# Round 0 of a fused attention and MLP kernel, taken in two parts of 128 and 256 steps

## Chip, core and metric

The kernel runs on one core of one Trainium2 chip. The metric is the device time of one execution in microseconds. TensorE multiplies matrices, VectorE and ScalarE work elementwise and read its results out of PSUM, GpSimd (POOL in the profile) does elementwise work on SBUF, and SyncE (SP) issues most of the transfers.

## The reference

Two blocks one after the other. The first is a linear attention with a decay per channel (batch 4, 8 heads, 768 steps, 48 channels a head), the second a norm and an MLP with a residual:

```python
for t in range(S):
    kt, vt, rt, wt = (k[:, :, t], v[:, :, t], r[:, :, t], w[:, :, t])
    cur = np.einsum('bhd,bhe->bhde', u[None] * kt, vt)
    y[:, :, t] = np.einsum('bhd,bhde->bhe', rt, state + cur)
    state = wt[:, :, :, None] * state + np.einsum('bhd,bhe->bhde', kt, vt)
x = y.transpose(0, 2, 1, 3).reshape(B, S, H * D)      # 4 x 768 x 384
xn = (x - mu) / np.sqrt(var + 1e-06) * g_ln           # mu, var over the 384
out = x + np.maximum(xn @ w_ch1, 0.0) @ w_ch2         # 384 -> 1536 -> 384
```

All inputs and the output are float32.

## The kernel before

**Rounds.** The work is cut into eight rounds of 384 steps, two for each batch entry; the second continues the state of the first. A round has two units (`uu`) of four heads, and the heads of a unit go in two pairs: two heads of 48 channels share the 128 partitions, at rows 0 and 64. The 384 steps are three tiles of 128 (`TT = 3`), each of two chunks of 64.

**Attention of a round** (`front`). `load` fetches `w`, `k` and `r` with steps on partitions. `turn` transposes them on TensorE (`w_ps`, `k_ps`, `r_ps`) and ScalarE, in round 0 also VectorE, copies them to SBUF with channels on partitions. `totals` multiplies decays together by halves, 64 steps to 1 chunk, in six instructions (`tot`, `decay`). Then six levels follow. At level `lev`, `quads` multiplies keys by queries for the blocks of size 2^lev (tile `a`), `keep` copies the wanted squares of the result into `A` under a mask, and `grow` scales `k` and `r` by the decay of that level, so that the next level, or the states, can use them. Level n+1 can only start once `grow` of level n is done, so the levels of one round are a serial chain between TensorE and VectorE. After the last level, `turn_k` transposes the keys back (`kn_ps`), `states` multiplies them by `v` and VectorE scans over the chunks (`s`, `last`), `own` and `own_term` make the term with `u` (`rk`, `own`, `vo`), and `outputs` multiplies `A` by `v` and the states by `r`; VectorE adds both into `x`. `load_v` fetches `v` and makes a copy `vx` with its two halves of partitions exchanged.

**MLP of a round** (`back`). `normalize` takes mean and variance of each step, `turn_x` transposes the result (`xT_ps`) and ScalarE scales it into `xf`. `mlp` multiplies by `w_ch1` in twelve products (`h_ps`, three matmuls each), applies the relu, then multiplies by `w_ch2` into three output tiles (`o`). Round 0 does this in float32; later rounds use split factors in a faster format (`xhl`, `xd`, `wh`, `wl`, `d`), which `halve` makes from the weights. `convert` prepares each of 24 weight tiles from its raw form: three ScalarE instructions (into `w` or `ffn`, and `held` or `rest`) and two VectorE ones, a shift and a join (`CUSTOM_DVE_ANT_0` in the profile).

**What sets the order.** The work is not issued as the functions are called. Each `plan.add` registers one operation with its engine, an estimated cost, the tiles it reads and writes, and a priority (`pri`, smaller is sooner; `at(rnd, stage)` is 40 a round plus the stage). `Plan.order` runs a list schedule over these estimates and emits the instructions in the resulting order, engine by engine; each engine then executes strictly in that order. So every change of an operation's cost, size or priority can move other operations, in later rounds too. Some points matter below. An operation with `port` set is not placed beside one of the other of VectorE and GpSimd; every GpSimd operation has it. When the plan sees TensorE wait over 0.4 us in its first 90 us, it puts `idle` matmuls of zeros there, up to three times 128 columns each. Tiles come from a fixed number of homes by tag, and `banks` are PSUM banks.

In `before`, round 0 has all 384 steps as one piece; `quads` and `grow` are issued separately for the two units in this round only. Its loads are six transfers of 288 KB, each row 576 bytes, three on SyncE's queue and three on ScalarE's.

Of the kernel before, what the change touches and what calls it, by code (L numbers as in the profile page):

```python
# [9 lines left out]
F32 = mybir.dt.float32  # L10
# [55 lines left out]
class Plan:  # L66
# [31 lines left out]
    def add(self, eng, cost, fn, r=(), w=(), new=(), pri=0, lat=0.0, size=0, port=False, tiled=False, count=0):  # L98
        costs = {eng: cost} if isinstance(eng, str) else dict(zip(eng, cost))
        op = Op(len(self.ops), costs, fn, pri, lat, size, port or "POOL" in costs, tiled, count)  # L100
# [160 lines left out]
def kernel(  # L261
# [57 lines left out]
    def tile_(tag, name, shape, dtype=F32):  # L319
        if name in tiles:  # L320
            return tiles[name]
        if tag == "a":
            tiles[name] = a_homes[plan.place[name]]
            return tiles[name]
        if tag == "nat" and name.startswith("nat_"):
            tiles[name] = nat_homes[plan.place[name]]
            return tiles[name]
        pool = banks if tag == "b" else homes
        t = pool.tile(shape, dtype, tag=f"{tag}{plan.place[name]}", name=name)
        tiles[name] = t  # L330
        return t
# [11 lines left out]
    for q in both_units:  # L343
        plan.hold("vo", f"nat_r{q}")
        tile_("vo", f"nat_r{q}", [P, NH * ROW])
# [27 lines left out]
    for t in nat_homes:  # L373
        POOL.memset(t[:, NH * ROW :], 0.0)
# [33 lines left out]

    SRC = {"w": w, "k": k, "r": r}

    def load(nm, q, eng="SP", pri=None):
        b, f, g = units[q]
        name = f"nat_{nm}{q}"

        queue = SP if eng == "SP" else ACT

        def go():
            to = tile_("nat", name, None)
            if q // U < ROWS:
                queue.dma_start(  # L420
                    out=to[:, 0 : NH * ROW].rearrange("p (h x) -> p h x", h=NH),
                    in_=SRC[nm][b, ts(g, NH), ds(f * RN, RN)]
                    .rearrange("h (p c) d -> p h (c d)", p=P),
                )
                return
            for c in range(TT):
                queue.dma_start(
# [4 lines left out]
        if pri is None:  # L432
            pri = at(q // U, "wrk".index(nm))
        new = [] if nm == "r" and q in both_units else [("nat", name)]
        cost, size = (0.5, 0.8) if q // U < ROWS else (1.65, 1.2)
        plan.add(eng, cost, go, w=[name], new=new, pri=pri, lat=2.0, size=size)
# [4 lines left out]
    def turn(nm, q, pr, stage):  # L441
        rnd, uu = divmod(q, U)
        key = f"nat_{nm}{q}"
        name, ps = f"{nm}{rnd}", f"{nm}_ps{q}_{pr}"

        rows = rnd < ROWS

        def go():
            t = tile_("b", ps, [P, RN])
            for c in range(TT):  # L450
                if not rows:
                    both = by_tile(tiles[key])[:, c, ts(pr, 2)].rearrange("p j d -> p (j d)")
                    PE.transpose(t[0:PD, ts(c, P)], both[:, 0:PD], ident)
                    continue


                at_ = 2 * pr * ROW + c * D
                second, first = ds(at_ + ROW - HP, PD), ds(at_, HP)
                PE.transpose(t[0:PD, ts(c, P)], tiles[key][:, second], ident)
                PE.transpose(t[0:HP, ts(c, P)], tiles[key][:, first], ident)  # L460

        def keep(e="ACT"):
            to, ps_ = tile_(nm, name, [P, U, W])[0:PD, uu, ts(pr, RN)], tiles[ps][0:PD]
            if rows:
                to = to.rearrange("p (s c) -> p s c", c=TT)
                ps_ = ps_.rearrange("p (c s) -> p s c", c=TT)
            (DVE.tensor_copy if e == "DVE" else ACT.copy)(out=to, in_=ps_)

        new = [(nm, name)] if uu == pr == 0 else []
        plan.add(  # L470
            "PE", 0.66 if rows else 0.33, go, count=12 if rows else 6, r=[key, (name, uu, pr)], w=[ps],
            new=[("b", ps)] + new, pri=at(rnd, stage), lat=0.17,
        )
        plan.add(
            ("ACT", "DVE") if rnd == 0 else "ACT", (0.45, 0.5) if rnd == 0 else 0.45, keep,
            r=[ps], w=[(name, uu, pr)], pri=at(rnd, stage) + EVICT / 2,
        )

    def parts_of(name, us=both_units):
        return [(name, uu, pr) for uu in us for pr in pairs]  # L480

    def totals(rnd):
        tot, dec, wt = f"tot{rnd}", f"decay{rnd}", f"w{rnd}"
        sizes = [U * W >> (lev + 1) for lev in range(NLEV)]
        starts = [sum(sizes[:i]) for i in range(NLEV - 1)]
        costs = list(zip((1.0, 0.55, 0.4, 0.3, 0.25, 0.2), (1.5, 0.9, 0.58, 0.42, 0.34, 0.25)))
        for lev in range(NLEV):
            def go(e, lev=lev):
                if lev == 0:
                    tile_("tot", tot, [P, U * W])  # L490
                    tile_("decay", dec, [P, U * NM])
                pair = level_total(rnd, lev).rearrange("p (q two) -> p q two", two=2)
                BY[e].tensor_tensor(
                    out=level_total(rnd, lev + 1), in0=pair[..., 0], in1=pair[..., 1], op=ALU.mult
                )
            plan.add(
                EITHER, costs[lev], go,
                r=parts_of(wt) if lev == 0 else [(tot, lev)],
                w=[(tot, lev + 1)] if lev < NLEV - 1 else [dec],
                new=[("tot", tot), ("decay", dec)] if lev == 0 else [], pri=at(rnd, 6 + lev),  # L500
            )

    def level_total(rnd, lev):
        if lev == 0:
            return tiles[f"w{rnd}"].rearrange("p u t -> p (u t)")[0:PD]
        if lev == NLEV:
            return tiles[f"decay{rnd}"][0:PD]
        n = U * W >> lev
        return tiles[f"tot{rnd}"][0:PD, U * W - 2 * n : U * W - n]

    def own(q):
        rnd, uu = divmod(q, U)
        b, f, g = units[q]
        kk, kr = f"nat_k{q}", f"nat_r{q}"
        rk, o, row = f"rk{q}", f"own{rnd}", f"own_row{rnd}"
        rows = rnd < ROWS

        def parts():

            t = tile_("rk", rk, [P, NH * ROW])  # L520
            if rows:
                views = [
                    t_[:, 0 : NH * ROW].rearrange("p (h c d) -> p c h d", h=NH, c=TT)
                    for t_ in (tiles[kk], tiles[kr], t)
# [4 lines left out]
            return views + [u_bc[:, None, ts(g, NH)].broadcast_to([P, TT, NH, D])]  # L529
# [9 lines left out]
        def third():  # L539
            t = tile_("own_row", row, [P, TT, H]) if rows else tile_("own", o, [P, TT, H])  # L540
            DVE.tensor_reduce(
                out=t[:, :, ts(uu, NH)], in_=parts()[2], axis=AX.X, op=ALU.add,
            )

        to = row if rows else o
        plan.add(EITHER, (0.76, 1.5), first, r=[kk, kr], w=[rk], new=[("rk", rk)], pri=at(rnd, 20))
        plan.add(EITHER, (0.76, 1.68), second, r=[rk, "u_bc"], w=[rk], pri=at(rnd, 20))
        plan.add(
            "DVE", 0.72, third, r=[rk], w=[(to, uu)],
            new=[("own_row" if rows else "own", to)] if uu == 0 else [], pri=at(rnd, 20),  # L550
        )

    def own_by_tile(rnd):

        row, o, key = f"own_row{rnd}", f"own{rnd}", ("own_d", rnd)

        def out_():
            SP.dma_start(
                out=own_d[rnd].rearrange("(p c) h -> p (c h)", c=TT),
                in_=tiles[row].rearrange("p c h -> p (c h)"),  # L560
            )

        def back():
            SP.dma_start(
                out=tile_("own", o, [P, TT, H]),
                in_=own_d[rnd].rearrange("(c p) h -> p c h", c=TT),
# [3 lines left out]
            "SP", 0.4, out_, r=[(row, uu) for uu in both_units], w=[key], pri=at(rnd, 20),  # L570
# [3 lines left out]
            "SP", 0.45, back, r=[key], w=[(o, uu) for uu in both_units], new=[("own", o)],  # L574
            pri=at(rnd, 20), lat=2.0, size=0.4,
        )

    def quads(rnd, lev, us=both_units):
        n, name = 1 << lev, f"a{rnd}_{lev}"

        def go():
            if us[0] == 0:
                tile_("a", name, [P, 2, 512])
            to = tiles[name][:, :, 0 : W // 2].rearrange("s j (u k t) -> s j u k t", u=U, k=NK)
            for uu in us:
                K = tiles[f"k{rnd}"][:, uu]
                R = tiles[f"r{rnd}"][:, uu].rearrange("p (m q two n) -> p m q two n", m=NM, two=2, n=n)
                for c in range(NK):
                    for i in range(2):
                        for j in range(2):  # L590
                            m = 2 * c + i
                            rows = ds(HP * j, D)
                            PE.matmul(
                                to[ds(C * (i ^ j), C - n), j, uu, c]
                                .rearrange("s (q n) -> s q n", n=n),
                                K[rows, ds(m * C, C - n)], R[rows, m, :, 1, :],
                                start=True, stop=True,
                            )

        plan.add(  # L600
            "PE", 0.7 * len(us) * (C - n + 6) / (C + 6), go,
            r=parts_of(f"k{rnd}", us) + parts_of(f"r{rnd}", us),
            w=[(name, uu) for uu in us], new=[("a", name)] if us[0] == 0 else [],
            pri=at(rnd, 7 + 2 * lev), lat=0.17, tiled=True, count=96 * len(us),
        )

    def grow(rnd, lev, nm, us=both_units):
# [3 lines left out]
        def go():  # L611
            T = level_total(rnd, lev).rearrange("p (u q two) -> p u q two", u=U, two=2)
            T = T[:, us[0] : us[0] + nu].rearrange("p u q two -> p (u q) two")[:, :, 1 - i]
            X = tiles[name][0:PD, us[0] : us[0] + nu].rearrange(
# [890 lines left out]
```

## Time and profile before

| what | value |
|---|---|
| time, median of 3 runs | 541.24 us (539.26 to 542.72) |
| profiled execution | 544.78 us |
| its span | 543.1 us |
| granted TensorE clock over the span | 0.988 |
| busy: TensorE, VectorE, ScalarE, GpSimd | 525.5, 394.5, 266.2, 82.6 us |
| first `h_ps` matmul of round 0 on the chain that ended last | 62.73 us |
| moved by DMA | 55.84 MB |

The span runs from the first to the last event of the profiled execution; the time beside it also holds what lies around the span. Busy shares are of the whole span, while the start of the program and its middle have different limits, so the views by window and the chain of work in order of time say more than the shares. `idle` matmuls are counted as busy. In the groups, PEld is the loading of weights into TensorE, which runs beside its matmuls, and a float32 matmul that is no transpose appears as two records. All instructions have the same line, since one helper records them; they are told apart by tile.

### The profile page before, as it was taken

To read this page: it belongs to the slowest core of one execution; us is meant where nothing else is said; L and a number is where in the kernel's file an instruction comes from. 1 tells how busy PE (TensorE), PEld (TensorE's weight loads), DVE (VectorE), ACT (ScalarE), POOL (GpSimd) and SP (SyncE) were. 2 spreads that over 40 slices of the span, in tenths; PEclk is the share of its full clock that TensorE was granted. 3 is DMA by queue.
4 is the path that set the end of the run, shared out by engine and by line. 5 is a ranking of instruction groups with operands and counts; after the bars stand their busy time and mean duration, and the time that the engine had idled before them with its cause. 6 is when DMAs were issued, how large, how long until landed. Compare 5 with 4: busy or idle time off the path is not lost.

```text
span 543.1 us, 20415 instructions
## 1 busy us (share of the span) xinstructions
PE 525.5 (97%) x8930; PEld 430.0 (79%) x8930; DVE 394.5 (73%) x805; ACT 266.2 (49%) x579; POOL 82.6 (15%) x112
## 2 busy tenths in 40 slices
PE   8979999999999999999799999999999999999995
PEld 7767666776797867799676799668866999999994
DVE  6886899889969888899676487634764866756554
ACT  4777887751563462553631583245831434333321
POOL 2313112431211321410400010001500000000000
PEclk9997999999999999999999999999999999999998
DMA  9975864278456527266120234013201312213201
GB/s 277 246 197 124 224 174 79 68 168 228 92 116 128 146 65 144 45 143 149 58 64 18 68 92 109 30 36 95 68 16 57 104 59 70 92 59 96 64 2 43
DMA packets 118841, 55.84 MB, mean 103 GB/s; under 512 B 86880, under 2 KB 115680, under 8 KB 118752
## 3 DMA queue, kind: packets, MB, share of 16 engines
q1 hardware_dynamic: 117168, 53.65, 38.9%
q8 instruction: 70, 1.15, 0.9%
q10 hardware_dynamic: 1584, 0.88, 0.6%
q14 instruction: 19, 0.16, 0.1%
HBM read 45.05 MB, written 7.10 MB: 96 GB/s over the span
## 4 chain that ended last, share of the span: by engine, by line
PE 81%; DVE 6%; DMA 4%; ACT 3%; SPq 3%; issue 2%; POOL 1%; POOLq 0%; DVEq 0%; ACTq 0%
PE a L49 22%; PE o L49 21%; PE h_ps L49 18%; PE hd_ps L49 7%; SPq L49 3%; PE r_ps L49 2%; PE w_ps L49 2%; PE o_2P L49 2%; PE k_ps L49 2%; PE kn_ps L49 2%; DMA nat<-in_r_dram 2%; DVE x L49 2%; PE idle L49 1%; PE xT_ps L49 1%; DMA raw<-in_moe_w_ch_dram 1%
## 5 line engine op out<-in xcount | busy, mean ns | idle before, releaser
L49 PE MATMUL o<-ffn,h 128*128 128x384 f32 x360 | 124.6, 490 | 0.0
L49 PEld LDWEIGHTS o<-ffn,h 128*128 128x128 f32 x360 | 65.5, 190 | 37.2
L49 ACT COPY h<-hd_ps 128x384 f32<-128x384 f32 x84 | 40.3, 479 | 91.0 <-PE hd_ps L49 89.3
L49 PEld LDWEIGHTS a<-r,k 48*56 48x56 f32 (+5 forms) x4608 | 64.4, 127 | 18.3 <-issue 10.4
L49 DVE SCALAR_TENSOR_TENSOR h<-h_ps,h 128x384 f32<-128x384 f32 x84 | 46.6, 556 | 42.1 <-PE h_ps L49 41.7
L49 PE MATMUL a<-r,k 48*56 48x32 f32 (+5 forms) x4608 | 70.3, 213 | 1.9 <-issue 1.5
L49 PE MATMUL h_ps<-xhl,wl 128*128 128x384 f32 x252 | 61.9, 354 | 0.6 <-ACT r L49 0.2
L49 PE MATMUL h_ps<-xhl,wh 128*128 128x384 f32 x252 | 57.9, 337 | 0.0
L49 PE MATMUL hd_ps<-xd,d 128*128 128x384 f32 x252 | 57.0, 351 | 0.0
L49 DVE TENSOR_TENSOR k<-k,tot 112x768 f32<-112x768 f32 (+1 forms) x45 | 39.8, 883 | 20.4 <-PE a L49 13.1
L49 PEld LDWEIGHTS h_ps<-xhl,wl 128*128 128x128 f32 x252 | 43.5, 188 | 4.6 <-ACT h L49 1.1
L49 PEld LDWEIGHTS hd_ps<-xd,d 128*128 128x128 f32 x252 | 44.0, 188 | 2.1
L49 PEld LDWEIGHTS h_ps<-xhl,wh 128*128 128x128 f32 x252 | 45.4, 188 | 0.0
L49 ACT ACTIVATE h<-h 128x384 f32<-128x384 f32 x48 | 25.0, 525 | 33.2 <-DVE h L49 32.7
L49 DVE COPY_PREDICATED A<-mask,a 128x768 f32<-128x768 int8 x32 | 38.4, 1208 | 3.0 <-PE a L49 3.0
L49 DVE TENSOR_TENSOR r<-r,tot 112x768 f32<-112x768 f32 (+1 forms) x45 | 40.1, 891 | 0.0
L49 ACT ACTIVATE hH<-h 128x384 fp32r<-128x384 f32 x36 | 18.8, 525 | 41.1 <-DVE h L49 41.1
L49 DVE SCALAR_TENSOR_TENSOR hL<-h,hH 128x384 fp32r<-128x384 f32 x36 | 20.0, 556 | 14.2 <-ACT hH L49 14.0
L49 POOL TENSOR_TENSOR vo<-v,own 128x576 f32<-128x576 f32 x13 | 15.3, 1178 | 88.8 <-DVE x L49 63.3
L49 ACT COPY A<-a 32x384 f32<-32x384 f32 x32 | 15.0, 468 | 27.7 <-PE a L49 25.7
L49 POOL TENSOR_TENSOR rk<-rk,u_bc 128x576 f32<-128x576 f32 x12 | 17.6, 1466 | 64.2 <-DVE ffn L49 18.9
L49 PE MATMUL a<-w2d,hD 128*128 128x384 f32 x72 | 25.5, 355 | 0.8 <-DVE hD L49 0.7
(118 smaller groups left out, 1007.7 us busy)
## 6 DMA issues: line engine op xcount, KB each, us to landing
d<-w1d SPq DMA_DIRECT2D x84, 192.0 KB, 2.8
raw<-in_moe_w_ch_dram SPq DMA_DIRECT2D x24, 384.0 KB, 4.5
v<-in_v_dram SPq DMA_DIRECT2D x48, 96.0 KB, 3.0
out_dram<-x SPq DMA_DIRECT2D x24, 192.0 KB, 1.9
nat<-in_w_dram SPq DMA_DIRECT2D x36, 96.0 KB, 3.0
nat<-in_k_dram SPq DMA_DIRECT2D x36, 96.0 KB, 3.0
nat<-in_r_dram SPq DMA_DIRECT2D x36, 96.0 KB, 3.0
vx<-v SPq DMA_DIRECT2D x32, 72.0 KB, 3.3
```

Of the source, the lines that this page charges most:

```text
L49: ins = self.tc.keep_in_program_order(f(*args, **kw))
```

## The change

Round 0 is cut into two parts: the first tile of 128 steps and the other two, 256 steps. Each function of `front` and of the norm takes a part `(rnd, c0, nc)`, first tile and number of tiles, instead of a round. `front`, `norm` and the first MLP product run over part 0, then over part 1; the second product (`mlp`) follows for the whole round. Later rounds are one part as before. Tiles keep their sizes; a part writes its columns of them, and the keys of the plan name the part. The states of part 1 continue those of part 0.

Operations of part 0 have the priority of a round earlier (`urgent`). Part 0 handles all eight heads in one instruction in most places: one load for each of `w`, `k` and `r` (192 bytes a row), one set of transposes for four pairs, and a copy of 512 columns. Part 1's loads have 384 bytes a row, and its pairs go two at a time. The first h product of each of the twelve is split into one with 128 columns and one with 256.

Around this: the masks of the levels have an earlier priority and no longer `port`; the load of `g` has an earlier priority; the shift and join of the first six weight tiles too; more of round 0's natural tiles have a home from the start, so the memsets of their margins differ; and PSUM tiles are allocated at a full bank and cut to size.

```diff
+    def parts_of_round(rnd):
+        return [(rnd, 0, TT)] if rnd else [(0, 0, 1), (0, 1, TT - 1)]
+
+    def urgent(part, stage):
+        rnd, c0, nc = part
+        return at(rnd - (nc == 1), stage)
...
+    def load_first(nm, part, eng, pri):
+        _, c0, nc = part
+        b, f = rounds[0]
+        name = natural(nm, part, 0)[0]
+        queue = SP if eng == "SP" else ACT
+        row, margin = row_of(part)
+
+        def go():
+            queue.dma_start(
+                out=tiles[name][:, margin : margin + H * row].rearrange("p (h x) -> p h x", h=H),
+                in_=SRC[nm][b, :, ds(f * RN + c0 * P, nc * P)]
+                .rearrange("h (p c) d -> p h (c d)", p=P),
+            )
...
+    def first_product(part):
+        rnd, c0, nc = part
+        steps = slice(c0 * P, (c0 + nc) * P)
+        for f in range(FC):
+            h_, ps, g, cols = f"h{rnd}_{f}", f"h_ps{rnd}_{f}_{c0}", f // G, ts(f % G, P)
+
+            def go(f=f, ps=ps, g=g, cols=cols):
+                t = tile_("b", ps, [P, nc * P])
+                for kc in range(KC):
+                    PE.matmul(
+                        t, tiles[f"w1_{g}"][:, kc, cols], tiles[f"xf{rnd}_{kc}"][:, steps],
+                        start=kc == 0, stop=kc == KC - 1,
+                    )
...
         pri = CONVERT + i / 100
+        first = -6 if i < FC // 2 else pri
...
-        plan.add("DVE", 0.32, shift, w=[key], pri=pri, port=True)
-        plan.add("DVE", 0.56, join, r=[rest_], w=[key], pri=pri, port=True)
+        plan.add("DVE", 0.32, shift, w=[key], pri=first, port=True)
+        plan.add("DVE", 0.56, join, r=[rest_], w=[key], pri=first, port=True)
...
             for i, nm in enumerate("wkr"):
-                for q, eng in zip(qs, ("SP", "ACT")):
-                    load(nm, q, eng, i)
-        if rnd == 0:
+                load_first(nm, part, ("SP", "ACT")[(i + c0) % 2], at(c0 - 1, i))
+        if rnd == c0 == 0:
...
-    front(0)
-    for i in range(len(parts)):
-        convert(i)
-    back(0)
+    for part in parts_of_round(0):
+        front(part)
+        norm(part)
+        if part[1] == 0:
+            for i in range(len(parts)):
+                convert(i)
+        first_product(part)
+    mlp(0)
```

The functions between (`turn`, `totals`, `own`, `quads`, `grow`, `keep`, `keep_last`, `exchange_r`, `turn_k`, `load_v`, `own_term`, `states`, `outputs`, `normalize`, `turn_x`) do what they did, on the columns of the part. In the emitted order, TensorE's rows go from transposing part 0, through its six levels with transposes of part 1 and of round 1 between them, to the first h product; part 1's levels, round 1's transposes and the other h products of part 0 alternate after that.

## The prediction

> **What bounds the kernel now.** I read the page from the top. The engine rows and the slices come first:
>
> ```profile
> PE 525.5 (97%) x8930; PEld 430.0 (79%) x8930; DVE 394.5 (73%) x805; ACT 266.2 (49%) x579; POOL 82.6 (15%) x112
> PE   8979999999999999999799999999999999999995
> PEclk9997999999999999999999999999999999999998
> ```
>
> TensorE looks full everywhere, with one dip and one loss of clock in the first tenth. But the plan fills its waits with `idle` matmuls that count as busy, so the share proves nothing there. The view that separates them is the chain that ended last, in order of time. From 62.7 us on every piece of it is a TensorE piece with work in it; before that it jumps between engines:
>
> ```profile
> 35.41 0.56 DVE k L49
> 35.97 0.46 DVE r L49
> 36.42 0.04 issue
> 36.47 0.97 DVE A L49
> 37.43 0.53 issue
> 37.96 2.34 PE kn_ps L49 x12
> 40.30 3.70 PE a L49 x144
> 44.00 4.53 PE idle L49 x8
> ...
> 59.34 1.27 DVE xn L49 x3
> 60.61 0.05 issue
> 60.65 0.99 PE xT_ps L49 x7
> 61.64 1.08 PE idle L49 x4
> 62.73 9.68 PE h_ps L49 x30
> ```
>
> Round 0 is one serial pass (level, copy, level, states, norm) with nothing else to multiply, and the dense stretch begins only with its first `h_ps`. The windows, third, show the two resources on either side of that point (columns: window and length; busy us of PE, PEld, DVE, ACT and POOL, each with its count; clock; DMA share; GB/s):
>
> ```profile
> 35.00:40.00 5.00, 2.40 (x54) 2.27 (x40) 4.53 (x7) 2.92 (x8) 1.47 (x1) 0.81 0.44 128
> 40.00:45.00 5.00, 5.00 (x148) 4.38 (x147) 2.57 (x11) 4.79 (x11) 0.83 (x2) 0.50 0.06 6
> 45.00:50.00 5.00, 5.00 (x72) 2.91 (x73) 2.81 (x13) 3.17 (x7) 3.16 (x3) 0.66 0.70 157
> 70.00:75.00 5.00, 5.00 (x110) 3.49 (x109) 5.00 (x11) 4.32 (x10) 0.00 (x0) 1.00 0.54 167
> 95.00:100.00 5.00, 5.00 (x117) 3.68 (x117) 4.58 (x8) 4.76 (x13) 0.00 (x0) 1.00 0.24 75
> ```
>
> The 2.6 us gap ending at 37.96 is followed by about ten microseconds of half clock (0.50). And from 70 us VectorE is as full as TensorE, so it stands next in line.
>
> **TensorE's ledger.** From its first transpose (4.37) to its first `h_ps` (62.73) lie 58.4 us. Work in them, by the warm rows: 72 transposes of round 0, 72 of round 1 and 6 of round 2, at 0.109 us (6 take 0.66), 16.4; six levels of round 0, 1.5 us falling to 0.95 (96 records each), 8.0; level 0 of round 1, 1.5; twelve `kn_ps`, 1.4 (the warm row is 1.36); states 1.2, outputs 2.7 and `xT_ps` 1.0. Sum 32.2, so **26.2 us are not work**: fillers, waits, half clock. That is the most the change can reach for.
>
> **The change, part by part.**
>
> *Part 0 ahead.* A third of round 0 (128 steps, eight heads) runs all six levels, states, outputs and norm first. Walk, from rows: `w` lands about 4.0 (before, 4.24); 8 transposes 0.9; the copy of 112x512 about 0.6 (112x384: 0.48). VectorE's four big memsets are as before and end at 6.44; six totals then cost 1.3, because 112x768 advances VectorE 0.87 us and 112x384 0.47, so 0.07 fixed and 1.04 ns per element: 256 elements, 0.34. Level 0 starts near 7.9, behind eight transposes of the second part, and takes 0.5 (a third of 1.5). VectorE then has 9.4 us of instructions in its new order up to the last `r` scaling; with about 1.0 of waits for TensorE that is 18.8. The tail: `kn_ps` and its copy 1.45; states 0.6; scan 0.8; swaps 0.8; outputs and their adds 1.55; statistics, root, reciprocal and `xn` 2.05; transposes and three scalings 1.45: 8.7. First `h_ps` at **27.5 us instead of 62.7**. TensorE's work until then is 15.4 (84 transposes 9.2; levels 4.2; the rest 2.0), so 8.1 us are not work. The new order has 36 filler units of 128 columns after the first transpose, 7.8 us at 0.216 each (a 384-column record takes 0.323), which agrees.
>
> *Part 1 behind it.* 256 steps. From here TensorE has h products of part 0, 60 transposes of round 1 and part 1's own levels: enough to be dense. VectorE is not so free. I summed its new order, instruction by instruction with the rates above (masked copies 0.9 for 768 elements, 1.8 at level 1; shift and join of a weight tile 0.39 and 0.47), to the last scaling of round 1: **76.5 us**. The old order's sum to the same instruction is 78.3, of which 3.2 belong to work the new order puts later: 75.1. Splitting costs 1.4 us, because the fixed 0.07 is small. In the old run that instruction ended at 97.9, so 19.6 us were waits and contention. In the new order I count 3.3 up to part 0's `xn` (23.1 of work, 26.4 on the clock), 5 for part 1's tail (`kn_ps`, states, swaps and outputs, which fillers on VectorE cover in part) and 2 for sharing with POOL (two weight instructions stretched from 0.35 to 1.19 and from 0.56 to 0.86 there). That gives about 87, and TensorE's level 5 of round 1 at 87.3 instead of 95.1 to 96.0 end to end; I take 96.0 against 87.3: 8.7 ahead. TensorE by its own ledger could be there near 77, so **VectorE sets this point**. Off it go 0.8 us of work (half an h product, three transposes) that now stands behind the point, and 1.0 because 3.2 us of VectorE work is still due there and the next ten microseconds before had 3.4 us of VectorE idle to take it. **Net: 6.9 us less.**
>
> *Half-width products.* 36 h matmuls of 384 columns become 36 of 128 and 36 of 256. The nearest row streams 384 columns in 0.323 per pass, two passes per matmul; thirds of it are 0.108 and 0.216, so nothing is added, if the weight load stays hidden. [...] The row that has both in one instruction is `xT_ps`: nine transposes with a 128x128 load each and 128 columns moved take 0.99 us, 0.11 each. I take 0.11 to 0.12, up to 0.9 us, and VectorE's lead over TensorE at that stage covers it; uncovered it is 0.9.
>
> *Smaller loads.* Rows of 192 and 384 bytes replace 576, and the DMA is full from 3 to 15 us (shares over 1.0), so this is no free edit. [...] Priced like 512-byte packets (28 ns in this trace), part 0's 3072 packets over 16 engines take 5.4 us; but the trace's 192-byte packets take 15 to 16 ns, so 3.1, against 2.3 for the same bytes in 576-byte packets of 36 ns. [...]
>
> *Queues.* Round 0 keeps six loads. SyncE gains four `vx` issues (0.7 to 0.9 us each, 3 us), and `g` (1.5 us) moves ahead of the second part's `k` and the weight tiles, whose issues slip from 3.25 to about 5.6. ScalarE converts its first weight tile at 14.3 now, so this is covered by some microseconds. Behind the `v` and `vx` issues round 1's `k` load lands near 19, and TensorE meets its `k_ps` just before the states, near 18.8: 0 to 1 us at risk, kept in the range. POOL: masks no longer wait for VectorE (`wide` waited 13.8 and 4.1 us for it in the first 60), which frees POOL and not the chain. ScalarE gets 12 more relus and smaller copies, about 3 us of fixed costs on an engine 49% busy.
>
> **Sum.** The profiled execution took 544.78 (span 543.1, 1.7 around it), 3.5 above the median 541.24. 544.78 - 6.9 = 537.9 in its terms; on the median, **534.3**.
>
> **Rivals.**
>
> 1. *VectorE keeps nearly all of it.* Its waits stay near the old 19.6 minus a few: part 1's levels wait for TensorE, which holds h products and transposes of 0.66 us in between, or another gap like that at 35.4 drops the clock. For it: VectorE was 97% full from 60 to 100. Against: the old waits sit in the serial pass. With 5 us more waits the gain is 1.9: 539.3.
> 2. *Dense from 27.5.* Only the 8.1 us remain: 26.2 - 8.1 = 18, less 0.9: 524. Against: VectorE's sum above.
> 3. *Slower: weight loads not hidden behind 128-column passes.* Place: `h_ps` of part 0, TensorE. Price 13.7 if load record and pass follow each other; 6.9 - 13.7 makes 548. It decides from 0.204 us per pass (6.9/72 above 0.108). For it: load records of 191 ns where transposes have 140. Against: the 0.11 per transpose.
> 4. *It doesn't do what it says*: the first h products start early, but wait for weight conversions, so TensorE has nothing dense. In the new order only f = 0 comes before part 1's levels; the rest are spread through it. This is part of rival 1.
>
> **How the numbers follow.** Forecast 0.52 (its own range 530 to 538), rival 1 with 4 0.22, rival 2 0.08, rival 3 0.18. One per cent, 5.4 us, is about what a measurement of this kernel can tell from no change. Four fifths of the forecast's chance (0.42) and rival 2 lie beyond it: faster 0.50; the rest of the forecast and rival 1: same 0.32; slower 0.18. The range takes the forecast, rival 1 with the DMA rule's 1.5 and the `k` load's 1 us, and most of rival 2: 525 to 543.
>
> **What would show it.** Right: first `h_ps` between 26 and 30 us; its 128-column passes near 0.11; level 5 of round 1 ending near 87; idle fillers under 10 us; VectorE near full from 27 to 90. Wrong: half clock for more than ten microseconds in the first 60, TensorE gaps with VectorE as releaser between 40 and 90 (rival 1), passes over 0.2 us (rival 3), or a late dense stretch that loses the lead again after 100 us, which nothing in my sum contains.

## The result, and the profile after

| | before | after |
|---|---|---|
| median of 20 runs | 541.82 us (539.08 to 546.31) | 537.98 us (535.59 to 540.66) |
| profiled execution, its span | 544.78, 543.1 us | 537.31, 535.4 us |
| granted TensorE clock over the span | 0.988 | 0.995 |

The ratio after to before is 0.9949, 95% interval 0.9928 to 0.9970. Between the medians of all runs the kernel became faster by 3.8 us; the ratio, which is not the quotient of these two medians, puts the gain between 1.6 and 3.9 us. Forecast were 6.9: the right direction, about half the size or less. The two profiled executions alone would have said 7.5.

The rows of the page that answer to those shown of before, engine totals and slices:

```profile
PE 521.3 (97%) x8994; PEld 434.4 (81%) x8994; DVE 403.2 (75%) x845; ACT 269.0 (50%) x602; POOL 73.0 (14%) x106
PE   8999899999999999999999999999999999999995
PEclk9999989999999999999999999999999999999999
```

A slice is 13.4 us here. The dip of the third slice is gone, and a smaller one with a loss of clock has come in the fifth and sixth, 54 to 80 us. The chain that ended last, in order of time, has the first `h_ps` at 33.47 instead of 62.73. TensorE's work carries it on to 53.8 us; from there it walks through VectorE, ScalarE and SyncE's queue to a load that TensorE waits for, a stall that was not there before:

```profile
22.59 0.75 DVE w L49 x2
...
23.47 0.84 DVE w L49 x2
...
33.47 0.86 PE h_ps L49 x6
34.34 1.03 PE a L49 x64
...
44.45 0.67 PE h_ps L49 x6
...
61.98 0.61 SPq L49
62.63 4.93 DMA nat<-in_k_dram
67.69 0.50 PE k_ps L49 x2
...
69.54 2.56 PE h_ps L49 x6
...
76.45 1.30 PE h_ps L49 x6
```

The six `h_ps` records of 128 columns at 44.45 take 0.67, 0.112 each; the six of 256 columns at 69.54 take 2.56, twice the 1.30 of those at 76.45, because the clock was 0.50 from 68.75 to 72.16. The windows show both ends of the change (columns as before):

```profile
35.00:40.00 5.00, 4.95 (x148) 4.17 (x140) 4.62 (x11) 4.35 (x10) 1.01 (x1) 1.00 0.91 255
40.00:45.00 5.00, 4.73 (x137) 4.10 (x130) 4.19 (x11) 4.12 (x10) 0.00 (x0) 1.00 0.99 298
45.00:50.00 5.00, 5.00 (x110) 4.40 (x111) 4.31 (x16) 4.22 (x12) 1.47 (x1) 1.00 0.34 89
65.00:70.00 5.00, 2.63 (x14) 2.08 (x14) 4.86 (x7) 1.91 (x5) 0.00 (x0) 0.88 0.78 168
70.00:75.00 5.00, 5.00 (x111) 4.14 (x111) 0.64 (x2) 3.41 (x9) 0.00 (x0) 0.78 0.74 186
```

Summed from 35 to 50 us, TensorE is busy 14.7 us instead of 12.4, VectorE 13.1 instead of 9.9, ScalarE 12.7 instead of 10.9 and GpSimd 2.5 instead of 5.5, and the clock is full. From 65 to 75 TensorE waits for a load of round 2's `k`, then VectorE waits in turn. SyncE's queue says why the load is late: it stands behind copies and weights.

```profile
58.81 0.34 SPq L49 DMA_DIRECT2D raw<-in_moe_w_ch_dram  x1
59.27 1.25 SPq L49 DMA_DIRECT2D vx<-v  x2
60.57 0.59 SPq L49 DMA_DIRECT2D raw<-in_moe_w_ch_dram  x1
61.34 1.25 SPq L49 DMA_DIRECT2D vx<-v  x2
62.63 1.80 SPq L49 DMA_DIRECT2D nat<-in_k_dram  x3
```

The place that it is loaded to came free at 58.9, when GpSimd's `rk` had read the round before; in before, the same load was issued at 46.38.

A ledger of TensorE's span for all kernels of this study, summed from the traces: gaps between its records, `idle` fillers (all lie in the first 80 us), and the rest, which is work including what half clock adds to it. The last 5.2 us of each span, after TensorE's last record, stand in no column. The ratio is to the kernel before, run on the same chip.

| kernel | gaps to 80 us | fillers | gaps after 80 | rest | span | ratio, interval |
|---|---|---|---|---|---|---|
| before | 6.2 | 16.5 | 6.2 | 509.0 | 543.1 | |
| before, second profile (E1) | 5.3 | 16.0 | 4.5 | 509.1 | 540.0 | 0.9999, 0.9971 to 1.0026 |
| before, gap filled (E2) | 6.1 | 14.3 | 6.6 | 510.8 | 543.0 | 1.0031, 1.0000 to 1.0063 |
| after | 6.0 | 11.5 | 3.0 | 509.8 | 535.4 | 0.9949, 0.9928 to 0.9970 |
| loads due earlier (E3) | 6.7 | 11.5 | 7.6 | 513.4 | 544.3 | 1.0081, 1.0047 to 1.0116 |
| k transposes due later (E4) | 6.7 | 11.5 | 10.2 | 513.6 | 547.2 | 1.0152, 1.0105 to 1.0199 |
| k transposes moved by hand (E5) | 6.9 | 11.5 | 4.2 | 511.2 | 539.0 | 0.9988, 0.9959 to 1.0018 |
| warm start (E6) | 5.7 | 12.4 | 3.1 | 510.7 | 537.1 | 0.9939, 0.9910 to 0.9969 |
| no second joins (E7) | 6.3 | 11.5 | 4.3 | 511.9 | 539.2 | 0.9945, 0.9911 to 0.9978 |
| E5 and E6 (E8) | 6.8 | 12.2 | 4.1 | 508.3 | 536.6 | 0.9948, 0.9914 to 0.9981 |

### The profile page after: what moved, and what is told of

Same layout as the page of the kernel before. It is cut to its first block, busy times and chain, and to the rows that moved or that the text cites. A ratio compares the mean times of both kernels' runs of the same rounds, so it can differ in the third digit from the quotient of the medians.

```text
span 535.4 us, 20629 instructions
## 1 busy us (share of the span) xinstructions
PE 521.3 (97%) x8994; PEld 434.4 (81%) x8994; DVE 403.2 (75%) x845; ACT 269.0 (50%) x602; POOL 73.0 (14%) x106
## 4 chain that ended last, share of the span: by engine, by line
PE 85%; DVE 7%; DMA 2%; issue 1%; POOL 1%; SPq 1%; ACT 1%; DVEq 0%; POOLq 0%; ACTq 0%
PE a L49 24%; PE o L49 21%; PE h_ps L49 18%; PE hd_ps L49 7%; PE w_ps L49 3%; PE k_ps L49 2%; PE r_ps L49 2%; PE o_2P L49 2%; PE kn_ps L49 2%; DVE x L49 2%; PE xT_ps L49 2%; PE idle L49 1%; DVE k L49 1%; PE o_2D L49 1%; DVE r L49 1%
## 5 line engine op out<-in xcount | busy, mean ns | idle before, releaser
L49 PEld LDWEIGHTS o<-ffn,h 128*128 128x128 f32 x360 | 65.4, 190 | 37.6
L49 PEld LDWEIGHTS a<-r,k 48*60 48x60 f32 (+5 forms) x4608 | 63.1, 126 | 19.6 <-issue 8.5
L49 PE MATMUL a<-r,k 48*60 48x32 f32 (+5 forms) x4608 | 69.4, 212 | 2.0 <-DVE r L49 1.3
L49 DVE TENSOR_TENSOR k<-k,tot 112x768 f32<-112x768 f32 (+1 forms) x50 | 41.4, 828 | 29.0 <-PE a L49 18.6
L49 PE MATMUL h_ps<-xhl,wl 128*128 128x384 f32 x252 | 60.8, 349 | 0.3
L49 PE MATMUL hd_ps<-xd,d 128*128 128x384 f32 x252 | 55.4, 347 | 0.0
L49 DVE COPY_PREDICATED A<-mask,a 128x768 f32<-128x768 int8 (+2 forms) x36 | 39.3, 1092 | 0.9 <-PE a L49 0.9
L49 ACT ACTIVATE hH<-h 128x384 fp32r<-128x384 f32 x36 | 18.8, 526 | 41.0 <-DVE h L49 41.0
L49 POOL TENSOR_TENSOR vo<-v,own 128x576 f32<-128x576 f32 (+1 forms) x12 | 13.5, 1121 | 141.3 <-DVE x L49 107.3
L49 ACT COPY w<-w_ps 112x384 f32<-112x384 f32 (+1 forms) x31 | 14.3, 489 | 34.3 <-PE w_ps L49 34.0
L49 DVE SCALAR_TENSOR_TENSOR hL<-h,hH 128x384 fp32r<-128x384 f32 x36 | 20.0, 555 | 14.3 <-ACT hH L49 14.0
L49 ACT COPY A<-a 32x384 f32<-32x384 f32 (+2 forms) x36 | 15.6, 433 | 27.8 <-PE a L49 27.5
L49 PE MATMUL h_ps<-xf,w 128*128 128x128 f32 (+1 forms) x144 | 27.7, 343 | 0.1
```

Of the source, the lines that this page charges most:

```text
L49: ins = self.tc.keep_in_program_order(f(*args, **kw))
```

## The experiments

Two theories stood at the start. T1: the stall at 65.4 us took some 4.5 us of a gain that was otherwise there. T2: VectorE's work sets the pace of that stretch, as the prediction had it. Beside them a doubt about the yardstick: the profile of before was longer than most of its runs.

**E1. The kernel before, profiled again** (no edit).

> The kernel before, unchanged, profiled a second time. Its profiled execution so far took 544.78 us, 3 us more than the median of its runs, while the profile of the changed kernel lies at the median of its own. Theory A (the first profile of before was a long one by chance, so the 7.5 us that the trace shows between the two kernels overstates the gain): this profile is near 542 us and lacks the TensorE gaps of 0.66, 1.88 and 0.54 us at 258 to 265 us. Theory B (profiling always lengthens this kernel by 3 us): 544 to 545 us again, with those gaps. The ratio of its timed runs is 1.000 within 0.002.

541.69 us, so theory A, though of the three gaps one stays, 0.97 at 257.5. VectorE's instructions, set side by side in their order, show where the first profile was longer. At 40 us it is 0.9 us ahead of the second, at 60 it is 2.6 behind; some 1.6 of that are given back by 258 us, and 2.3 are lost again between 258 and 262, where a load of `r` comes late. The second profile's chain, in the stretch on which the prediction's ledger was built:

```profile
37.72 1.34 PE kn_ps L49 x12
39.06 3.56 PE a L49 x144
42.62 4.06 PE idle L49 x8
...
60.12 1.95 PE h_ps L49 x6
```

The gap ahead of `kn_ps` is 1.50 us here instead of 2.60, the half clock after it some 6.8 us instead of 10.2, and the first `h_ps` comes at 60.12 instead of 62.73. Against this profile the change is worth 541.69 - 537.31 = 4.4, near the 3.8 of the medians. Its span is 4.6 longer than after's; in the ledger, 3.8 of that are gaps and fillers up to 80 us and 1.5 gaps after it, less 0.7 more work in after.

**E2. Before, with the gap at 35.4 filled.**

```diff
             t = tile_("b", ps, [P, RN])
+            for _ in range(4 if q == pr == 0 else 0):
+                PE.matmul(t, zeros, nought.broadcast_to([P, RN]), start=True, stop=True)
             for c in range(TT):
```

> The kernel before with four filler products of 128x384 in TensorE's order ahead of the first k transposes of round 0, to keep TensorE busy through the 2.60 us gap at 35.4 us which is followed by 10.24 us of half clock (38.1 to 48.4). If the gap and its half clock set the end of before's fill (and so part of what the change takes away), the half clock goes and the time falls by 2 to 5 us, to 537 to 540. If VectorE sets the fill (rival), the half clock costs nothing there: 541 to 543, the same as before.

The half clock is gone (1.00 in every window of 2 us from 34 to 62, 0.998 over the span), and at the end nothing was gained. TensorE reaches the next late thing sooner and waits there 1.06 us, for the `k` load of round 2:

```profile
46.90 0.43 SPq L49
...
47.38 4.04 DMA nat<-in_k_dram
51.42 0.14 issue
51.56 0.29 PE k_ps L49
```

So keeping the clock up did not shorten the kernel. That does not make the half clock free: the four fillers cost 2.6 us by themselves, and VectorE's instructions, side by side, still run 2.1 us ahead of before's first profile at 60 to 75 us. Of that lead 1.9 are left at 105, 0.9 at 250 and 0.1 at the end: in the order of before, two microseconds won in round 0 were lost again in later rounds.

**E3. After, round 2's loads due earlier.** The order is planned anew.

```diff
-            "SP", cost_, go, w=[name], new=[("nat", name)], pri=at(q // U, "wrk".index(nm)), lat=2.0,
+            "SP", cost_, go, w=[name], new=[("nat", name)], pri=at(q // U, "wrk".index(nm)) - 60 * (q // U == 2), lat=2.0,
```

> The changed kernel with the loads of round 2's natural tiles given an earlier due time, so that in SyncE's queue they stand ahead of the v and vx loads of the second part, which wait for outputs. Theory T1 (the k load stuck behind them costs the gap of 2.30 us at 65.4 us, the half clock of 3.41 us after it, and with both some 4.5 us of the end): the gap goes or falls under 1 us, no half clock from 60 to 80 us, time 533 to 535. Rival T2 (VectorE sets the rate of these 30 us and makes up for it whatever TensorE does): gap gone, time 537 to 538.5. Rival T3 (the home that the load waits for comes free only at 58.9 us, and the loads behind it now wait longer): a gap elsewhere, 537 to 540.

**E4. After, round 2's k transposes due later.** Planned anew.

```diff
-            pri=urgent(part, stage), lat=0.17,
+            pri=210 if (nm, rnd) == ("k", 2) else urgent(part, stage), lat=0.17,
```

> The changed kernel with the transposes of round 2's k given a later due time, so that in TensorE's order the first products of the second part stand ahead of them; the load is where it was. T1 (a stall in a fixed order: only what is queued behind the late load suffers): the gap of 2.30 us and the half clock after it go, time 533 to 535.5. T2 (VectorE sets the rate): 537 to 538.5. If the later walk of round 2 costs as much: 538 to 541.

Both missed, to the other side: 547.77 and 550.56 us. In E3 the gap at 65 is gone and the same kind of wait stands further on, for the second unit's `k` (timeline of TensorE):

```profile
72.83 0.29 PE L49 MATMUL k_ps<-ident,nat 128*112 128x128 f32 x1 [0.77 <-DMA nat<-in_k_dram]
74.96 1.31 PE L49 MATMUL k_ps<-ident,nat 128*112 128x128 f32 x5 [1.83 <-DMA nat<-in_k_dram]
```

But the 8.9 us by which E3's span is longer than after's do not lie there: gaps up to 80 us differ by 0.7, gaps after 80 by 4.6, the rest by 3.6. One due time in round 2 gave another order for the rounds behind it. E4's largest single loss is at 230 us, and has nothing to do with `k` of round 2. TensorE waits for VectorE's scaling of `k`, and in VectorE's order a product `rk` stands ahead of it, which by the profile waited 6.2 us for a transfer of split weights (`d<-w1d`):

```profile
234.94 1.35 PE L49 MATMUL kn_ps<-ident,k 112*128 112x112 f32 x6 [4.89 <-DVE k L49]
```

In E4, too, the wait near 65 us only moved: TensorE waits 1.66 and 0.80 us for `w` of round 2 at 68.6 and 70.5. Neither run says what the stall costs. What they show is that the plan is more sensitive than the change: by their ratios they are 1.3 and 2.0% slower than after, for one number in a priority. The last four runs therefore keep after's finished order, with nothing planned anew: E5, E6 and E8 move or add rows in it by hand, and E7 leaves instructions out.

**E5. The finished order of after, late transposes moved.** On TensorE, with the copies that follow them, the order in words (`h` is a product of part 1, `a` a level):

```diff
-w_ps, k_ps, w_ps, k_ps (unit 0); h 1; w_ps x2 (unit 1); a (level 2 of round 1); h 2; k_ps x2 (unit 1); h 3; r_ps; a (level 3); r_ps; h 4; h 5; h 6
+w_ps x2 (unit 0); h 1; h 2; a (level 2 of round 1); k_ps x2 (unit 0); w_ps x2 (unit 1); h 3; a (level 3); h 4; k_ps x2 (unit 1); h 5; h 6; r_ps x2
```

> The changed kernel with its finished order kept as it is, row for row, and one edit made in that order afterwards: from 65 to 78 us the transposes of round 2 that wait for late loads (the two units' k, the second unit's w, the first r) stand behind the h products and levels that they held up. Unlike the two runs before, nothing is planned anew. T1 (the stall at 65.4 us and its half clock cost some 4.5 us of the end): the gap is under 0.5 us, no half clock from 60 to 80 us, level 5 of round 1 ends near 86 instead of 90.4, time 533 to 535. T2 (VectorE sets the rate and makes up for the stall): 537 to 538.5. T4 (the lead is there at 90 us, and waits further on take it back): level 5 near 86, but 535.5 to 538.

A miss: 540.26 us, ratio 0.9988, an interval that only just meets after's. The gap at 65 is gone and 2.21 us of gap stand at 75.02. VectorE's timeline shows the way:

```profile
73.04 0.55 DVE L49 CUSTOM_DVE_ANT_0 ffn<-ffn,rest 128x768 uint16<-128x768 uint16 x1
74.65 0.36 DVE L49 TENSOR_SCALAR ffn<-ffn 128x384 int32<-128x384 int32 x1 [1.06 <-ACT ffn L49]
75.75 0.56 DVE L49 CUSTOM_DVE_ANT_0 ffn<-ffn,rest 128x768 uint16<-128x768 uint16 x1 [0.74 <-ACT rest L49]
76.23 0.95 DVE L49 TENSOR_TENSOR r<-r,tot 112x768 f32<-112x768 f32 x1
```

The level needs `r<-r,tot`. In VectorE's order a weight tile's shift and join stand ahead of it; these wait for ScalarE's conversions; and ScalarE's conversions stand behind the copies of `k_ps` and `w_ps`, which came late because the load did (ScalarE was idle 2.37 us there for TensorE). So the lateness passes from TensorE to ScalarE, to VectorE and back. This profile also started 1.4 us later than after's (below), and the levels of round 1 end at 93.47 instead of 90.38. From 105 us to the end the two kernels run in step: E5 is behind by 3.1 us at 105 and by 3.6 at 418. With after's order, what was lost in the first 100 us stayed.

**E6. The finished order of after, two more filler units at the start.** The order in words:

```diff
-  idle 128x384, idle 128x256
+  idle 128x384 x2, idle 128x128
   w_ps (part 0)
```

> The changed kernel with its order kept row for row, and two more filler units of 128 columns among the idle products at the very start, to close the gap from 3.5 to 4.4 us before the first transposes, which ran at the cold clock (1.93 us for eight where 0.9 was predicted). If part 0's walk sets the end of the fill, as the prediction's step from 27.5 to the end had it for TensorE: first h_ps 1 to 1.5 us earlier (32 instead of 33.5), time 536.5 to 537. If part 0 has slack against VectorE and the late loads (rival): first h_ps earlier and time 537.5 to 538.5. If the clock needs longer than that to rise: nothing moves.

537.51 us, ratio 0.9939. Against after's 0.9949 the intervals overlap, so no gain is shown. TensorE's timeline at the start:

```profile
0.99 3.36 PE L49 MATMUL idle<-nought 128*128 128x384 f32 x6 [0.99 <-DVE eps L49]
4.33 1.62 PE L49 MATMUL w_ps<-ident,nat 128*112 128x128 f32 x8
5.79 1.04 PE L49 MATMUL k_ps<-ident,nat 128*112 128x128 f32 x8
```

and after's own:

```profile
4.42 1.93 PE L49 MATMUL w_ps<-ident,nat 128*112 128x128 f32 x8 [0.93 <-POOL wide L49]
6.14 1.62 PE L49 MATMUL k_ps<-ident,nat 128*112 128x128 f32 x8
```

With the 0.93 us filled, the second group of eight takes 1.04 us, which in after only the third does. It isn't felt, because a load is next in line: `k` of round 1 lands at 23.5, TensorE waits 0.79 us for it, and `h_ps` begins at 33.5 as in after. The time is that of the rival, the first `h_ps` is not. The chain of E6:

```profile
19.99 3.52 DMA nat<-in_k_dram
23.52 0.14 issue
23.65 0.84 PE k_ps L49 x6
```

**E7. The order of after, VectorE's joins for `w_ch2` left out** (twelve instructions, 6.7 us; this kernel leaves out a part of the weights).

```diff
             bits = value_().bitcast(I32)
+            if i >= FC:
+                return
             DVE.tensor_tensor(out=bits, in0=bits, in1=tiles[rest_].bitcast(I32), op=ALU.add)
```

> The changed kernel with the same order, but VectorE's joins of the twelve tiles of w_ch2 are left out (12 instructions of 0.56 us, 6.7 us of VectorE between 45 and 90 us; the output differs). T2, the prediction's own step (VectorE sets level 5 of round 1): level 5 ends 3 to 6 us earlier and the time is 533 to 535. T1 (the chain through the late k load sets it): the gap at 65.4 us stays, level 5 at most 1.5 us earlier, 536.5 to 538.

538.57 us, ratio 0.9945: T2 falls. VectorE has 6.7 us less to do, and no gain is shown; one of some 2 us could hide in the two intervals, the 3 to 5 of T2 could not. Level 5 of round 1 ended at 92.64, not 3 to 6 us before after's 90.38 but later: the stall is longer here. VectorE's waits up to 93 us, summed from the traces, rise from 14.5 to 22.8. Its largest waits there (columns: sum, times, longest), in E7:

```profile
DVE k L49 <- issue: 6.7, 1, 6.7
DVE k L49 <- PE a L49: 5.8, 9, 2.4
DVE ffn L49 <- ACT ffn L49: 4.8, 7, 1.4
```

and in after:

```profile
DVE k L49 <- issue: 4.4, 1, 4.4
DVE k L49 <- PE a L49: 3.8, 7, 1.0
```

The 4.4 and the 6.7 are the stall behind the `k` load (TensorE's gap there is 2.30 in after and 3.42 in E7, and 3.41 and 6.83 us of half clock follow). The scaling of `k` ahead of it begins at 66.4 in both: the joins were not in its way. The edit is not quite clean: GpSimd's `decay` of round 1 came at 64.35 instead of 59.51; what reads it comes after level 5.

**E8. E5 and E6 together.**

> Both edits of the order of the changed kernel together, the late transposes moved behind the products and the two filler units at the start. T1 with slack in part 0: as the first of them alone, 533 to 535. If the two add: 532 to 534. T2: 537 to 538.5.

538.23 us, ratio 0.9948, the same as after. The first eight transposes take 1.06 us here, the gap at 65 is gone, and 2.21 us of gap stand at 74.14, as in E5, this time with no half clock behind it. No version of this study is shown to beat after.

## Why the prediction was right or wrong

**The step that failed is the lead at level 5 of round 1, 96.0 - 87.3 = 8.7 us, and with it "VectorE sets this point".** The level's last piece on TensorE, in before, in its second profile (E1) and in after:

```profile
95.14 0.95 PE a L49 x66
92.83 0.95 PE a L49 x66
89.42 0.95 PE a L49 x66
```

It ends at 96.09, 93.78 and 90.38. So the lead is 5.7 us against the first profile and 3.4 against the second. Of the 8.7, 2.2 belonged to the first profile alone, and 3.1 were missing because after came to this point at 90.4 instead of 87.3. Behind it the sum erred the other way: it took 1.8 off, and the lead grew by 1.2 instead, to the 4.6 between the spans of E1 and after. 6.9 - 2.2 - 3.1 + 3.0 = 4.6. The last term, the later rounds, was in no part of the sum. Gaps after 80 us fell from 4.5 (6.2 in the first profile) to 3.0; kernels that keep after's order have 3.0 to 4.3 there, so some of it is chance too, and its cause stays open.

**Why after came late: TensorE had no slack.** The prediction let TensorE be there at 77 and VectorE at 87. In after TensorE worked 53.6 of the 56.9 us from its first `h_ps` to the end of level 5, with no filler among them. Of its 3.3 us of gaps VectorE ended 0.46 by the profile, and the load of round 2's `k` 2.30:

```profile
63.36 1.56 PE L49 MATMUL a<-r,k 48*62 48x32 f32 x96 [0.46 <-DVE r L49]
67.69 0.87 PE L49 MATMUL k_ps<-ident,nat 128*112 128x128 f32 x3 [2.30 <-DMA nat<-in_k_dram]
```

From 77 to 90.4 its own sum grew by 6.0 (first `h_ps` at 33.5 instead of 27.5), 3.3 of gaps, 1.7 of half clock (3.41 us at half speed) and 2.4 that no row here places. E7 agrees: leaving out 6.7 us of VectorE's work shows no gain. VectorE's own term was mis-sized as well: 10.3 us of waits were counted beside 76.5 of instructions, and the last scaling of that level ended at 92.55, so 16.0 lay beside them (by the trace, 78.1 busy and 14.5 idle). One wait, 4.36 us to 74.42, is most of the difference. It comes from the `k` load of round 2, which the prediction didn't look at; it saw the risk for round 1's `k`, where E6 shows 0.8 us.

**From the profile to the median.** The prediction took 6.9 off 544.78, which gave 537.9 for a profiled execution, and then took the 3.5 between that profile and the median off as well, to 534.3. The profile after took 537.31, but it lies 0.7 below the median of its own kernel, where the profile of before lay 3 above its: the offset belonged to one execution, not to the kernel. E1 shows it with 541.69. Part of the 3.1 us between the two profiles arose between 40 and 60 us, in the stretch that the change rebuilds, so the 26.2 us of "not work" were summed from a pass that ended 2.6 us later than the second one. Another part arose near 260, where the prediction had not looked: its chain stops at 130 us, and the statement that every later piece is TensorE's doesn't hold for the whole chain (TensorE has 81% of it, and the first 62.7 us are only 12% of the span). That 537.9 met 537.31 is luck: errors that cancel.

**T1, the theory formed after the result, isn't borne out either.** Taking the late transposes out of TensorE's way moved the gap and returned no time (E5, E8), since the same lateness came back through ScalarE and VectorE. Open is what the load itself costs: a kernel with only SyncE's queue changed, the two loads ahead of the `vx` copies, was not run.

**The prediction's own list of signs.** Right: 128-column passes take 0.112 to 0.12 us, beside load records of 191 ns in after as in before, so the weight loads stay hidden (rival 3, whose 13.7 us were 72 loads of 0.19 us one behind the other, is dead; `xT_ps` was the right row to go by); from 20 to 60 us the clock was full; the smaller loads delayed part 0 by 0.3 us at most (a wait for `r` in E8). No run shows the 1.5 us that the range adds for the DMA; the runs show those 0.3 in their place. In part: fillers fell from 16.5 to 11.5, where under 10 was expected, and VectorE was near full but for a hole from 70 to 75 us (0.64 of 5). Missed: the first `h_ps` came at 33.5 instead of 27.5. The first transposes ran at about half their later pace (1.93 us for the first eight where 0.9 was put, 1.04 for the third eight) and level 0 started at 9.4 instead of 7.9; the last `r` scaling ended at 22.6 instead of 18.8; and the tail took 10.9 instead of 8.7. The tail's sum left out that the change puts the shift and join of the first weight tiles earlier: the chain has them on VectorE from 22.59 to 24.51, ahead of part 0's states. As TensorE has almost no gap after its first `h_ps`, these 6 us should count nearly in full; no run isolates them. One reading of before was too high: VectorE from 60 to 100 us is 94% full by the windows, not 97%.

Rival 1 comes closest in size (539.3), and half of its mechanism came true: another stall with a loss of clock, and VectorE waiting. But a DMA ended the wait, not VectorE.

## What to carry to other kernels

Profile the kernel before twice and compare the two traces first: where they differ in the very stretch that a change rebuilds, a ledger of its waits carries that difference, and the profile's offset from the median need not carry over to the changed kernel. In a kernel whose order is planned from priorities, an edit of a priority tests the plan and not the mechanism; fix the finished order and move rows by hand. An engine that is over 90% full in a stretch need not set its pace: look whose gaps it ends, then leave some of its work out and see whether anything moves.

## What was not expected of the hardware

The half clock came in lengths that are multiples of one: 3.41 us in after and E5, 6.83 in E1 and E7, 10.24 in before, after gaps of 2.30, 2.21, 1.50, 3.42 and 2.60 us. The same gap of 2.21 in E8, and one of 1.65 in E2, were followed by none. So the length didn't follow the gap. The stretches of full clock are multiples as well: 30.72 us in before and E1 are nine times 3.413, the 61.44 of after 18 times, the 68.27 of E5 20 times. In the clock records of before and after every stretch between two changes is such a multiple: 30.72, 10.24 and 491.52 us in before (9, 3 and 144 times), 61.44, 3.41 and 460.80 in after (18, 1 and 135 times).

Where these changes fall against the program isn't fixed. In the eight profiles with the same two fillers at the start the first record of full clock begins between 7.3 us (after) and 10.5 (E3), a spread of 3.2 us. With the same start, part 0's three groups of eight transposes took 1.93, 1.62 and 1.04 us in after, and 1.93, 1.91 and 1.91 in E5, and E5's first `h_ps` came 1.4 us later (34.8 against 33.4). The column "rest" of the ledger goes along with it: from 508.3 in E8 (full clock from 3.9, no half clock) over 509.8 in after to 511.9 in E7 (full clock from 10.0, 6.83 us of half clock). One profile carries chance of this size, most of what the change is worth.
